# One kernel, one change: gate and value products of batch 0 on 16-bit parts, and the scores of a pair's first two row blocks issued in one run

## The chip, the cores and the metric

The kernel runs on one core of a Trainium2 chip. Its engines are TensorE (PE, whose weight loads the profile lists apart as PEld), VectorE (DVE), ScalarE (ACT), GpSimd (POOL) and SyncE (SP, whose queue issues the transfers). The metric is the time of one execution in device microseconds, the median of several runs.

## What is computed

Four batches of 576 tokens, 8 heads of 64. Inputs are 32-bit floats, and the result must hold about that precision.

```python
scores = q @ k.T / 8, causal;  a = softmax(scores);  local = a @ v
phi(x) = where(x > 0, x, exp(x) - 1) + 1
mem = (phi(q) @ M_prev) / (phi(q) . z_prev + 1e-6)
x  = g * mem + (1 - g) * local              # g = sigmoid(beta) per head; 512 columns
h  = (x @ w1) * (x @ w2)                    # 1024 columns
x2 = (h @ w3) @ moe_w_out                   # 512 columns
y  = (sigmoid(x2 @ w_gate) * (x2 @ w_val)) @ moe2_w_out   # 1536 columns inside, 512 out
```

## The kernel before

**Stages.** For each batch, `attention(b)` makes x, and `ffn(b)` goes through four stages that the trace calls `ab` (x times w1 and w2, f = 0 to 7), `xw` (h times the product of w3 and w_out, which is made once at the start, `wps`; d = 0 to 3), `gv` (gate and value, f = 0 to 11) and `ot` (output). Attention of batch b+1 is interleaved with `ffn(b)`: `drive` (L1376) steps the attention generator at the `yield`s of the feed-forward loops. The `gv` loops have no `yield` inside, so no attention is interleaved there. PE's order is the order in which the program issues (`manual_schedule`, L1441); the other engines' orders, and SP's, come from a scheduler that simulates the program.

**Precise products.** A 32-bit matrix is split into a high part and the rest, and each block product is three matmuls (high x high, low x high, high x low; `prod`, L519). In batch 0 all parts are 32-bit (`split_rows`, L720: a cast on ACT, a subtraction on DVE). From batch 1 on, gate and value use 16-bit parts that are scaled by a power of two first (`split_scaled`, L178: ACT makes the high part, DVE the low one). The power comes from the largest magnitude: `largest` gives maxima per partition, `total` (L168) adds these over the partitions by a matmul with a matrix of ones, and `power` (L158) takes four small DVE steps from it. Batches 2 and 3 use a scheme with fewer products (`two_rows`), for which sums of weight blocks are prepared too.

**Weights.** They arrive as 64-bit words. `conv_step` (L379) turns half a unit into 32-bit floats (two ACT passes and one on DVE), takes the maximum of gate/value, ab and o2 units, stores a 32-bit copy (`kept`; `kf`, `ko` in the trace) and issues the load of the half three further on. A unit of gate and value is the 8 blocks of 128 x 128 for one f. `split_step` (L458) then splits a half into a slot of the ring `wslot` (five slots of 4 KB per partition). A unit of batch 0 so takes two slots. `conv_step` runs at most two units ahead of `split_step`. `pump` (L489) calls one late step, one `conv_step` and one `split_step` after every second block product of `prod`, that is after six matmuls.

**Late tasks.** When all units are converted, `late_step` works through `tasks` (L243): it reloads a kept copy (`wrawl`), makes the scaled 16-bit parts "P", the block sums, and their parts "S" (`late_split`, L321), and stores them for the batches to come. The list starts with the P parts of the 12 gate/value units, then the six of o2, then the eight ab units (P, sums, S), then the S parts of gate/value, then of o2. `limit` says how far the list may be worked in a stage, `pace` after how many pumps a piece is done. The scales of all these weights are made in one go after gate/value of batch 0 (`late_scales`, L311), o2's at the start of batch 1 (L762).

**Scores.** `s_part` (L1146) issues the scores of one row block i of a pair of heads, 116 rows by 116 (i + 1) columns, for both heads of the pair at once: three terms of two matmuls of 64 rows each, into the two PSUM banks "s", which DVE then reads with the mask and a running minimum (L1174). The fifth row block is done in two runs of 290 columns. After it come exp on ACT, the normalisation on DVE or POOL, and transposes into the one bank "t".

Of the kernel before, what the change touches and what calls it, by code (L numbers as in the profile page):

```python
# [32 lines left out]
PB = 5  # L33
# [30 lines left out]
def tile_attention_memory_ffn(  # L64
# [178 lines left out]
    tasks = [(u, "P") for u in jobs[:F2]] + [(("o", *x), "P") for x in pairs_of]  # L243
# [28 lines left out]
    ws = {"conv": 0, "step": 0, "split": 0, "ring": 0, "freed": 0, "use": 0, "again": 0, "pumps": 0, "late": 0, "task": 0, "part": 0, "limit": 0, "pace": 0, "tops": 0, "wo": 0, "pass": 0, "wready": False}  # L272
    tmp = {}

# [46 lines left out]
    def late_split():  # L321
# [5 lines left out]
        late_o2 = u not in rank  # L327
        by = o2s[:, 0:1] if late_o2 else wsc[:, rank[u] : rank[u] + 1]
# [50 lines left out]
    def conv_step():  # L379
# [27 lines left out]
        elif ws["step"] == 1:  # L407
# [7 lines left out]
            if u in rank:  # L415
# [42 lines left out]
    def split_step():  # L458
# [5 lines left out]
        u, hf = divmod(s, 2)  # L464
        r = raws[u][:, 4 * hf : 4 * hf + 4, :]
# [28 lines left out]
    def need(store, s):  # L494
        while s not in store:
            moved = split_step()
            moved = conv_step() or moved
            assert moved
# [216 lines left out]
    def gvw(b, s, w, k):  # L715

        m = (k + 2 * w) % 4
        return (slot(s), 4 * w + m) if b else (slot(s + w), m)

# [37 lines left out]
    def ffn(b):  # L757
# [3 lines left out]
        if b == 1:  # L761
            o2_scale()  # L762
            ws["limit"], ws["pace"] = NFIRST, PACE[5]
        if b == 2:
            ws["pace"] = PACE[3]
        if b > 0:
            htop = fp.tile([128, F1], F32, tag="htop", name=f"htop{b}", bufs=1)
        for f in range(F1):
# [36 lines left out]
            if b > 0:  # L805
                largest(htop[:, f : f + 1], hraw, AX.X)

# [11 lines left out]
        for d in range(KC):  # L819
            if b > 0 and d == 1:  # L820
                x2back = finish_x2(b, x2s)
                if b == 1:
                    split_scaled(x2[0][:, 0], x2[0][:, 1], x20, x2s[:, 0:1])
            s = take(2)
            if b < 2:
                xt = fp.tile([128, 2, S], F16 if b else F32R, tag=f"x{d}", name=f"x2_{b}_{d}", bufs=1)
                x2.append(xt)
            if b == 1 and d == 0:
                x20 = fp.tile([128, S], F32, tag="hraw", name="x20")
            for n, hf in enumerate((1, 0) if b > 1 and d == KC - 1 else (0, 1)):  # L830
                c0 = hf * HS
                ps = ps_f.tile([128, 512], F32, tag="f", name=f"xw{b}_{d}_{hf}")
# [7 lines left out]
                if b == 0:  # L840
                    nc.scalar.copy(xt[:, 0, c0 : c0 + HS], ps[:, :HS])
                    nc.vector.tensor_sub(
                        xt[:, 1, c0 : c0 + HS], ps[:, :HS], xt[:, 0, c0 : c0 + HS].bitcast(F32)
                    )
                elif b == 1 and d == 0:
                    nc.scalar.copy(x20[:, c0 : c0 + HS], ps[:, :HS])
                elif b == 1:
# [37 lines left out]
        if b == 1:  # L885
            ws["limit"], ws["pace"] = NPARTS, PACE[1]
# [14 lines left out]
        for f in range(F2):  # L901
# [41 lines left out]
            s = take(1 if b else 2)  # L943
            for hf in range(2):
                c0 = hf * HS
                pss = []
                for w in range(2):
                    ps = ps_f.tile([128, 512], F32, tag="f", name=f"gv{b}_{f}_{hf}_{w}")
                    pss.append(ps)
                    for k in range(KC):  # L950
                        prod(ps[:, :HS], *gvw(b, s, w, k), x2[k], c0, k == 0, k == KC - 1)
                        if k % 2 == 1:
                            pump()
                    if w == 0:
                        asb = fp.tile([128, HS], F32, tag="asb", name=f"gsb{b}_{f}_{hf}")
                        act_fn(out=asb, in_=ps[:, :HS], func=AF.Sigmoid, scale=x2back[:, f : f + 1] if b else 1.0)
                    if hf == 1 and (b == 0 or w == 1):
                        release(s + (w if b == 0 else 0))
                if b:
                    nc.vector.scalar_tensor_tensor(  # L960
                        hraw[:, c0 : c0 + HS], pss[1][:, :HS], x2back[:, f : f + 1], asb, ALU.mult, ALU.mult
                    )
                else:
                    nc.vector.tensor_mul(hraw[:, c0 : c0 + HS], pss[1][:, :HS], asb)
# [6 lines left out]
        if b == 0:  # L971
            late_scales()
            ws["limit"], ws["pace"] = F2, PACE[0]
# [59 lines left out]
    def finish_x2(b, x2s):  # L1033
        power(x2s[:, 0:1], x2s[:, 1:2], total(f"x2sum{b}", bcol[:, B + b : B + b + 1]))
        back = fp.tile([128, F2], F32, tag="x2back", name=f"x2back{b}", bufs=1)
        nc.vector.tensor_scalar(back, wsc[:, NJ : NJ + F2], x2s[:, 1:2], None, ALU.mult)
# [29 lines left out]
    def attention(b, lag):  # L1066
# [79 lines left out]
        def s_part(p, i, n):  # L1146
            w = T * (i + 1)
            if n == 0:
                ps_ = []
                for hh in range(2):  # L1150
                    name = f"p{b}_{p}_{i}_{hh}"
                    if first and np_["n"] % 2 == 0:
                        m = np_["n"] // 2 % P0
                        ps_.append(fp.tile([T, 2 * S], F32, tag=f"h{m}", name=name, bufs=1)[:, :SP])
                    else:
                        ps_.append(ap.tile([T, SP], F32, tag="p", name=name, bufs=PB))
                    np_["n"] += 1
                sp[p, i] = (ps_, ap.tile([T, 8], F32, tag="sm", name=f"sm{b}_{p}_{i}", bufs=6))
# [362 lines left out]
```

## Time and profile before

| What | Before |
|---|---|
| Median of three runs (lowest, highest) | 1017.32 us (1014.89, 1017.9) |
| The profiled execution's own time | 1013.13 us |
| Its span, from first to last instruction | 1011.3 us |
| PE busy, PEld busy | 97%, 79% of the span |
| DVE, ACT, POOL busy | 72%, 59%, 19% of the span |
| Transfers | 227 MB, 225 GB/s on average |
| Granted TensorE clock | 0.995 of full speed |

All positions are microseconds from the start of the span of one profiled execution. "Busy" of an engine is the time in which at least one of its instructions was running; overlapping ones count once. Durations of matmuls are longer than the distance from one to the next, since they are pipelined; the pace is read from the busy time of a group over its count. Stages of batch 0: `ab` from 117.9, `xw` from 219.1, `gv` from 257.3, `ot` from 334.1; of batch 1: `ab` from 385.7, `xw` to 499.5, `gv` to 570.3, `ot` to 622.

### The profile page before, as it was taken

Reading aid. Unit: us, or ns where it says so; the run is one execution under the profiler, and the core shown is the slowest. Engines: PE = TensorE matmul, PEld = TensorE weight load, DVE = VectorE, ACT = ScalarE, POOL = GpSimd, SP = SyncE. Lnnn points to the kernel's source line nnn. Section 1 sums busy time; section 2 is a strip of 40 time slices with the busy share of each in tenths; the row PEclk is TensorE's granted clock in tenths of the full one; section 3 lists DMA queues with packets and bytes.
Section 4 is the critical chain, followed back from the end, with each engine's and each line's share of the span. In section 5 each row is a group of like instructions: output and inputs, shape, how many; then the busy total and the mean of one; then the engine's idle time right before and its main releaser. Section 6 shows DMA issues by size and latency. Waiting matters only on the chain. (4 is left out here: it accounts for less than half of the span.)

```text
span 1011.3 us, 19894 instructions
## 1 busy us (share of the span) xinstructions
PE 982.4 (97%) x7351; PEld 797.9 (79%) x7351; DVE 731.3 (72%) x1702; ACT 596.6 (59%) x1213; POOL 195.0 (19%) x196
## 2 busy tenths in 40 slices
PE   7999999999999999999999999999999999999998
PEld 3556687888999898898977777778777667797776
DVE  6866788777778826777777668988876757737883
ACT  7987787567777735564654545555655545324451
POOL 3454012213000101312200011343111311201110
PEclk9989999999999999999999999999999999999999
DMA  8865799967777249877887576655655556556532
GB/s 293 245 230 192 247 346 310 326 206 254 249 250 247 98 137 380 286 226 238 297 310 261 176 251 240 214 190 184 200 181 178 185 157 204 186 174 246 183 131 79
DMA packets 95642, 227.21 MB, mean 225 GB/s; under 512 B 11192, under 2 KB 39992, under 8 KB 95288
## 3 DMA queue, kind: packets, MB, share of 16 engines
q1 hardware_dynamic: 95544, 225.93, 66.3%
q8 instruction: 58, 0.95, 0.4%
q14 instruction: 40, 0.33, 0.1%
HBM read 164.55 MB, written 61.34 MB: 223 GB/s over the span
## 5 line engine op out<-in xcount | busy, mean ns | idle before, releaser
L532 PEld LDWEIGHTS <-wslot 128*128 128x128 f16 x1680 | 162.9, 98 | 49.7 <-issue 8.3
L1200 POOL TENSOR_SCALAR p<-p,sm,omg 116x116 f32<-116x116 f32 (+4 forms) x100 | 89.0, 895 | 406.2 <-DVE sm L1198 294.9
L521 PE MATMUL gv<-x,wslot 128*128 128x288 f32 (+1 forms) x1152 | 147.5, 290 | 0.2 <-ACT gsb L137 0.2
L521 PEld LDWEIGHTS <-wslot 128*128 128x128 f16 x1152 | 111.1, 98 | 32.1 <-issue 4.5
L532 PE MATMUL gvp<-x,wslot 128*128 128x288 f16 x1008 | 125.2, 286 | 3.6 <-ACT x L180 1.6
L137 ACT ACTIVATE p<-p,sm 116x116 f32<-116x116 f32 (+4 forms) x160 | 93.2, 585 | 46.6 <-DVE sm L1174 46.5
L521 PE MATMUL ot<-hg,wslot 128*128 128x288 f16 (+1 forms) x864 | 118.1, 291 | 0.0
L521 PE MATMUL ab<-x,wslot 128*128 128x288 f32 x768 | 117.2, 302 | 0.5 <-ACT asb L800 0.3
L521 PE MATMUL xw<-h,wslot 128*128 128x288 f32 x768 | 113.0, 300 | 1.7 <-ACT h L721 1.0
L521 PEld LDWEIGHTS ab<-x,wslot 128*128 128x128 f32 x768 | 104.0, 188 | 6.3 <-issue 2.9
L521 PEld LDWEIGHTS xw<-h,wslot 128*128 128x128 f32 x768 | 103.4, 188 | 5.5 <-issue 2.0
L1174 DVE CUSTOM_DVE_ANT_0 p<-s,msk 116x116 f32<-116x116 f32 (+4 forms) x160 | 68.0, 452 | 30.8 <-PE s L1169 26.8
L532 PE MATMUL abp<-x,wslot 128*128 128x288 f16 x672 | 87.1, 286 | 1.3 <-DVE u2ab L603 1.1
L723 DVE TENSOR_TENSOR wslot<-wraw,wslot 128x512 fp32r<-128x512 f32 x76 | 54.9, 725 | 34.7 <-ACT wslot L721 34.4
L521 PEld LDWEIGHTS gv<-x,wslot 128*128 128x128 f32 x576 | 76.4, 188 | 0.5 <-ACT gsb L137 0.5
L1230 PE MATMUL t<-idf,p 116*116 116x116 f32 x480 | 68.7, 272 | 3.3 <-DVE p L1200 2.5
L1230 PEld LDWEIGHTS t<-idf,p 116*116 116x116 f32 x480 | 54.3, 139 | 18.0 <-issue 5.3
L402 ACT ACTIVATE cy<-r 128x512 f32<-128x512 f32 x76 | 51.5, 678 | 13.3 <-DVE wraw L411 2.6
L721 ACT CAST wslot<-wraw 128x512 fp32r<-128x512 f32 x76 | 47.1, 621 | 16.2 <-PE gv L521 7.4
L411 DVE SCALAR_TENSOR_TENSOR wraw<-cy,cr 128x512 int32<-128x512 int32 x76 | 54.2, 740 | 2.6 <-ACT cr L403 2.1
L521 PE MATMUL wps<-wo,wslot 128*128 128x512 f32 x192 | 52.2, 407 | 0.0
L1248 ACT COPY pt<-t 116x696 f32<-116x696 f32 (+2 forms) x74 | 47.5, 650 | 7.4 <-PE t L1230 7.1
(210 smaller groups left out, 1630.0 us busy)
## 6 DMA issues: line engine op xcount, KB each, us to landing
wslot<-k SPq DMA_DIRECT2D x40, 512.0 KB, 4.3
wslot<-ka SPq DMA_DIRECT2D x40, 512.0 KB, 4.4
wrawl<-kf SPq DMA_DIRECT2D x32, 512.0 KB, 6.1
wslot<-kb SPq DMA_DIRECT2D x40, 384.0 KB, 3.5
k<-wslot SPq DMA_DIRECT2D x24, 512.0 KB, 4.7
r<-in_gv_dram SPq DMA_DIRECT2D x24, 512.0 KB, 5.1
kf<-wraw SPq DMA_DIRECT2D x20, 512.0 KB, 3.5
ka<-wS SPq DMA_DIRECT2D x20, 512.0 KB, 4.4
```

Source lines behind the costliest of these rows:

```text
L137: ins = nc.scalar.activation(**kw)
L402: nc.scalar.activation(out=y, in_=hi, func=AF.Prelu, scale=2.0**-112, alpha=2.0**32)
L411: nc.vector.scalar_tensor_tensor(z, y, 3, tmp["r"], ALU.logical_shift_left, ALU.bitwise_or)
L521: paced["pe"] = nc.tensor.matmul(ps, w[:, wi, blk, :], x[:, xi, cols : cols + n], start=first and part == 0, stop=last and part == 2,)
L532: paced["pe"] = nc.tensor.matmul(ps, w[:, wi, blk + k, :], x[:, xi, k, :], start=not more and k == 0 and part == 0, stop=k == 1 and part == 2,
L721: nc.scalar.copy(dst[:, 0], src)
L723: eng.tensor_sub(dst[:, 1], src, dst[:, 0].bitcast(F32))
L1174: nc.vector.tensor_tensor_reduce(out=ps_[hh][:, c0:c1], in0=os_[hh], in1=msk[:, SP - w + c0 : SP - w + c1], scale=-0.125, scalar=3.0e38 if ...
L1200: lower(SHARE_N).tensor_scalar(ps_[hh][:, :w], ps_[hh][:, :w], sm[:, 6 + hh : 7 + hh], omg[:T, 2 * p + hh : 2 * p + hh + 1], ALU.mult, ALU ...
L1230: nc.tensor.transpose(tp[:T, c : c + T], src[hh][:, j * T : (j + 1) * T], idf[:T, :T])
L1248: nc.scalar.copy(to, got)
```

## The change

Gate and value units are now split once, at conversion, into scaled 16-bit parts of the whole unit: `scaled_step` waits until both halves are converted, issues the unit's own scale (`unit_scale`: two one-column products of ones into the bank "t", then `power`) at least four pumps after the last conversion, and at a later pump the split of all 1024 columns into one slot, whose store for the later batches is issued at once. The 12 P tasks of gate/value leave the late list, `late_scales` keeps only ab's scales, and o2's scale moves to the first late o2 task. x2 of batch 0 becomes scaled 16-bit parts as in batch 1: the bound on it needs a maximum of every h (two for each of the last four f) and the maxima of the w3-w_out product. Gate/value of batch 0 then runs as in batch 1 (one slot a unit, a scale in the sigmoid and in the product). In attention of batches 1 to 3, `s_part` issues row blocks 0 and 1 together, side by side in the same two banks, and returns at once for row block 1; score buffers become six, and q's tile gets a single buffer. The limits of the late list follow: o2's P parts during the output stage of batch 0, ab's parts from the start of batch 1, the S parts of gate/value from the gate/value stage of batch 1.

```diff
-PB = 5
+PB = 6
...
-    def total(name, *cols):
+    def total(name, *cols, bank=None):
         n = cols[0].shape[1]
-        ps = ps_f.tile([128, 512], F32, tag="f", name=name)
+        ps = (bank or ps_f).tile([128, 512], F32, tag="t" if bank else "f", name=name)
...
-    tasks = [(u, "P") for u in jobs[:F2]] + [(("o", *x), "P") for x in pairs_of]
+    tasks = [(("o", *x), "P") for x in pairs_of]
...
     def late_scales():
-        power(wsc[:, :NJ], wsc[:, NJ:], total("wsum", mcol[:, 0, :NJ], mcol[:, 1, :NJ]))
-        nc.vector.tensor_reduce(wmax, wtop.rearrange("p d f -> p f d"), AX.X, ALU.max)
+        power(wsc[:, F2:NJ], wsc[:, NJ + F2 :], total("wsum", mcol[:, 0, F2:NJ]))
...
+    def unit_scale(u):
+        n = rank[u]
+        power(wsc[:, n : n + 1], wsc[:, NJ + n : NJ + n + 1], total(f"wsum{n}", *(mcol[:, hf, n : n + 1] for hf in range(2)), bank=ps_t))
+        scaled.add(u)
+
+    def scaled_step(u, now):
+
+        if ws["conv"] < 2 * u + 2:
+            return False
+        if u not in scaled:
+            if not now and ws["pumps"] < ws["ready"]:
+                return False
+            unit_scale(u)
+            return True
+        if in_use("wslot") >= RING:
+            return False
+        w = fp.tile([128, 2, 8, 128], F16, tag="wslot", name=f"wslot{ws['ring']}", bufs=RING)
+        split_scaled(w[:, 0], w[:, 1], raws.pop(u), wsc[:, rank[u] : rank[u] + 1])
+        nc.sync.dma_start(out=whole16[u]["P"], in_=w)
+        done.append((u, "P"))
+        put("wslot", [w])
+        ws["split"] += 2
+        return True
...
+        if late_o2 and "o2" not in scaled:
+            scaled.add("o2")
+            o2_scale()
+            return
...
+                ws["ready"] = ws["pumps"] + 4
             ws["step"] = 0
             ws["conv"] += 1
...
+        if u in rank and rank[u] < F2:
+            return scaled_step(u, now)
...
         if b == 1:
-            o2_scale()
-            ws["limit"], ws["pace"] = NFIRST, PACE[5]
+            ws["limit"], ws["pace"] = NPARTS, PACE[5]
...
-            if b > 0:
+            if b > 0 or f >= F1 // 2:
                 largest(htop[:, f : f + 1], hraw, AX.X)
+            if b == 0 and f >= F1 // 2:
+                m = f - F1 // 2
+                largest(htop[:, m : m + 1], hs[m][:, 0].bitcast(F32), AX.X)
...
+                if b == 0 and d == 0 and n == 1:
+                    while ws["tops"] < KC:
+                        assert conv_step() or split_step()
+                    nc.vector.tensor_reduce(wmax, wtop.rearrange("p d f -> p f d"), AX.X, ALU.max)
+                    x2s = bound_x2(b, htop)
...
         if b == 1:
-            ws["limit"], ws["pace"] = NPARTS, PACE[1]
+            ws["limit"], ws["pace"] = NSUMS, PACE[1]
...
-            s = take(1 if b else 2)
+            s = take(1)
+            if b == 0:
+                slot(s)
+                nc.vector.tensor_mul(x2back[:, f : f + 1], wsc[:, NJ + f : NJ + f + 1], x2s[:, 1:2])
...
-            ws["limit"], ws["pace"] = F2, PACE[0]
+            ws["limit"], ws["pace"] = NFIRST, PACE[0]
...
-                q_ = ap.tile([128, NT, 2, D], F32, tag="qnr", name=f"qnr{b}_{p}")
+                q_ = ap.tile([128, NT, 2, D], F32, tag="qnr", name=f"qnr{b}_{p}", bufs=1)
...
+            if i == 1 and not first:
+                return
+            rows = (0, 1) if i == 0 and not first else (i,)
+            jobs = []
+            at = 0
+            for i in rows:
...
+                jobs.append((i, w, c0, c1, at))
+                at += c1 - c0
...
+            for i, w, c0, c1, at in jobs:
+                for x, (q_, k_) in enumerate(terms):
+                    for hh in range(2):
+                        r = slice(64 * hh, 64 * hh + 64)
+                        nc.tensor.matmul(
+                            os_[hh][:, at : at + c1 - c0], q_[r, 0, i * T : (i + 1) * T], k_[r, 1, c0:c1],
+                            start=x == 0, stop=x == len(terms) - 1,
+                        )
+            for i, w, c0, c1, at in jobs:
+                ps_, sm = sp[p, i]
                 for hh in range(2):
...
```

## Rows read from the trace of the kernel before

**Rows 1.** The page's part 1: busy us (share) x instructions, whole span

```profile
PE 982.4 (97%) x7351; PEld 797.9 (79%) x7351; DVE 731.3 (72%) x1702; ACT 596.6 (59%) x1213; POOL 195.0 (19%) x196
```

**Rows 2.** Busy time by stretch: length, PE, PEld, DVE, ACT, POOL, PEclk, DMA share, GB/s

```profile
174.00:219.00 45.00, 44.64 (x347) 40.25 (x346) 32.43 (x80) 26.18 (x59) 8.46 (x8) 1.00 0.78 267
219.00:257.30 38.30, 36.64 (x285) 32.59 (x284) 30.66 (x75) 26.79 (x58) 9.86 (x8) 1.00 0.75 261
257.30:334.10 76.80, 76.56 (x578) 76.26 (x578) 60.36 (x108) 58.25 (x110) 0.00 (x0) 1.00 0.72 244
334.10:385.70 51.60, 50.44 (x376) 46.51 (x374) 24.42 (x51) 24.94 (x44) 6.00 (x4) 0.97 0.41 137
385.70:499.50 113.80, 113.09 (x880) 101.21 (x878) 84.22 (x223) 67.96 (x146) 30.91 (x27) 1.00 0.82 279
499.50:570.30 70.80, 70.80 (x581) 56.57 (x580) 51.95 (x90) 39.43 (x55) 0.00 (x0) 1.00 0.81 270
570.30:622.00 51.70, 50.38 (x418) 37.35 (x417) 35.74 (x79) 26.64 (x46) 4.98 (x5) 1.00 0.63 210
498.00:515.00 17.00, 17.00 (x140) 13.82 (x139) 11.51 (x19) 9.21 (x13) 0.17 (x1) 1.00 1.04 365
```

**Rows 3.** Groups by form, whole span: busy us, mean ns | idle before

```profile
L521 PE MATMUL gv<-x,wslot 128*128 128x288 f32 x576 | 76.7, 295 | 0.2 <-ACT gsb L137 0.2
...
L521 PE MATMUL gv<-x,wslot 128*128 128x288 f16 x576 | 70.8, 286 | 0.0
```

**Rows 4.** Timeline of PE in batch 1's gate/value stage: start, us, what

```profile
517.15 0.17 PE L172 MATMUL hgsum<-bcol,ones 128*128 128x1 bf16 x1
517.18 0.65 PE L521 MATMUL gv<-x,wslot 128*128 128x288 f16 x4
```

**Rows 5.** DVE's groups by form, 257.3 to 334.1 (gate/value of batch 0)

```profile
L723 DVE TENSOR_TENSOR wslot<-wraw,wslot 128x512 fp32r<-128x512 f32 x24 | 16.5, 687 | 14.3 <-ACT wslot L721 14.3
L176 DVE TENSOR_REDUCE mcol<-wraw 128x1 bf16<-128x512 f32 x24 | 16.3, 680 | 0.0
L411 DVE SCALAR_TENSOR_TENSOR wraw<-cy,cr 128x512 int32<-128x512 int32 x24 | 15.4, 682 | 0.0
L964 DVE TENSOR_TENSOR hgraw<-gv,gsb 128x288 f32<-128x288 f32 x23 | 10.3, 448 | 2.1 <-ACT gsb L137 1.7 <-PE gv L521 0.4
L723 DVE TENSOR_TENSOR hg<-hgraw,hg 128x576 fp32r<-128x576 f32 x11 | 8.2, 747 | 0.0
```

**Rows 6.** Groups by form, whole span, of operations that batch 0 takes over

```profile
L181 DVE SCALAR_TENSOR_TENSOR wP<-wrawl,wsc,wP 128x1024 f16<-128x1024 f32 x12 | 15.7, 1305 | 11.6 <-ACT wP L180 11.0 <-DMA wslot<-k 0.5
...
L960 DVE SCALAR_TENSOR_TENSOR hgraw<-gv,x2back,gsb 128x288 f32<-128x288 f32 x24 | 12.4, 516 | 11.5 <-PE gv L521 9.6 <-PE hgsum L172 1.5 <-ACT gsb L137 0.4
```

**Rows 7.** Line 163, a step of `power`: duration ns min/median/max

```profile
L163 DVE TENSOR_SCALAR pw<-x2sum x3: 144/157/158, 475.5 to 893.6; 128x1 int32<-128x1 int32 x3
```

**Rows 8.** DMA issues by line: count, KB each, median us to landing

```profile
r<-in_gv_dram SPq DMA_DIRECT2D x24, 512.0 KB, 5.1
...
kb<-wP SPq DMA_DIRECT2D x12, 512.0 KB, 6.1
```

**Rows 9.** Timelines of PE around score visits in ab of batches 1 and 2

```profile
386.30 0.31 PE L1169 MATMUL s<-qkh 64*116 64x116 f32 x2
...
386.75 2.64 PE L521 MATMUL ab<-x,wslot 128*128 128x288 f32 x18
389.32 0.36 PE L1169 MATMUL s<-qkh 64*116 64x232 f32 x2
...
389.82 0.66 PE L521 MATMUL ab<-x,wslot 128*128 128x288 f32 x3
...
623.38 4.58 PE L532 MATMUL abp<-x,wslot 128*128 128x288 f16 x36
627.90 0.37 PE L1169 MATMUL s<-qkh 64*116 64x232 f32 x2
```

**Rows 10.** Timeline of PE in ot of batch 0, with [idle before <-releaser]

```profile
347.06 0.90 PE L1169 MATMUL s<-qkh 64*116 64x290 f32 x2 [1.16 <-DVE sm L1174]
```

More of the change, by code (lines that the diff above doesn't have):

```diff
@@ L271, in tile_attention_memory_ffn @@
     wot = {}
-    ws = {"conv": 0, "step": 0, "split": 0, "ring": 0, "freed": 0, "use": 0, "again": 0, "pumps": 0, "late": 0, "task": 0, "part": 0, "limit": 0, "pace": 0, "tops": 0, "wo": 0, "pass": 0, "wready": False}
+    ws = {"conv": 0, "step": 0, "split": 0, "ring": 0, "freed": 0, "use": 0, "again": 0, "pumps": 0, "late": 0, "task": 0, "part": 0, "limit": 0, "pace": 0, "ready": 0, "tops": 0, "wo": 0, "pass": 0, "wready": False}
     tmp = {}
+    scaled = set()
     last = {}
@@ L456, in load_step, with split_step @@
         return True
-    def split_step():
+    def split_step(now=False):
         s = ws["split"]
@@ L819, in ffn @@
         for d in range(KC):
[L820 removed]
+            if d == 1:
                 x2back = finish_x2(b, x2s)
[L822 removed]
+                if b < 2:
                     split_scaled(x2[0][:, 0], x2[0][:, 1], x20, x2s[:, 0:1])
@@ L955, in ffn @@
                         asb = fp.tile([128, HS], F32, tag="asb", name=f"gsb{b}_{f}_{hf}")
[L956 to L964, printed above, removed]
+                        act_fn(out=asb, in_=ps[:, :HS], func=AF.Sigmoid, scale=x2back[:, f : f + 1])
+                    if hf == 1 and w == 1:
+                        release(s)
+                nc.vector.scalar_tensor_tensor(
+                    hraw[:, c0 : c0 + HS], pss[1][:, :HS], x2back[:, f : f + 1], asb, ALU.mult, ALU.mult
+                )
             if b:
@@ L1159, in s_part @@
-            ps_, sm = sp[p, i]
-            c0, c1 = (0, w) if w <= 512 else ((0, SP // 2), (SP // 2, SP))[n]
-            os_ = []
-            for hh in range(2):
-                ps = ps_s.tile([128, 512], F32, tag="s", name=f"s{b}_{p}_{i}_{n}_{hh}")
-                os_.append(ps[:T, : c1 - c0])
-            terms = [(qks[p], qks[p])] if first else [(parts[p][x], parts[p][y]) for x, y in ((0, 0), (1, 0), (0, 1))]
-            for x, (q_, k_) in enumerate(terms):
-                for hh in range(2):
-                    r = slice(64 * hh, 64 * hh + 64)
-                    nc.tensor.matmul(
-                        os_[hh], q_[r, 0, i * T : (i + 1) * T], k_[r, 1, c0:c1],
-                        start=x == 0, stop=x == len(terms) - 1,
-                    )
@@ L1173, in s_part @@
-            for hh in range(2):
-                nc.vector.tensor_tensor_reduce(
-                    out=ps_[hh][:, c0:c1],
-                    in0=os_[hh],
-                    in1=msk[:, SP - w + c0 : SP - w + c1],
-                    scale=-0.125,
-                    scalar=3.0e38 if n == 0 else sm[:, 2 * hh : 2 * hh + 1],
-                    op0=ALU.add,
-                    op1=ALU.min,
-                    accum_out=sm[:, 2 * hh + n : 2 * hh + n + 1],
-                )
+            if i == 1 and not first:
+                return
@@ new lines, in s_part @@
+            os_ = [
+                ps_s.tile([128, 512], F32, tag="s", name=f"s{b}_{p}_{i}_{n}_{hh}")[:T, :at] for hh in range(2)
+            ]
+            terms = [(qks[p], qks[p])] if first else [(parts[p][x], parts[p][y]) for x, y in ((0, 0), (1, 0), (0, 1))]
+            for i, w, c0, c1, at in jobs:
+                for x, (q_, k_) in enumerate(terms):
+                    for hh in range(2):
+                        r = slice(64 * hh, 64 * hh + 64)
+                        nc.tensor.matmul(
+                            os_[hh][:, at : at + c1 - c0], q_[r, 0, i * T : (i + 1) * T], k_[r, 1, c0:c1],
+                            start=x == 0, stop=x == len(terms) - 1,
+                        )
```

60 lines of the change are left out of this document (31 added, 29 removed).

## The prediction

> **What bounds the kernel now.** I read the page's busy line first: TensorE is busy 982.4 of 1011.3 us [rows 1], so only what shortens or interrupts TensorE's own stream counts. Then the busy time by stage [rows 2]. In the gate/val stage of batch 0 (257.3 to 334.1) PE is busy 76.56 of 76.8 us, DVE 60.36, ACT 58.25, and the transfers run at 244 GB/s with a share of 0.72: it is PE-bound, but the other engines have only a fifth to spare. The same 576 products of batch 1 (499.5 to 570.3) fill 70.8 us, also without idle time. The groups by form say why [rows 3]: 576 products with 32-bit parts are 76.7 us of PE, 133 ns each; with 16-bit parts 70.8 us, 123 ns each.
>
> **Part 1, 16-bit gate/val products.** 76.7 - 70.8 = -5.9 us if nothing else stands in the way. Twelve scale sums of two one-column products are new in PE's stream; before such a product 0.03 us pass until the next big one starts [rows 4], so 12 x 2 x 0.03 = +0.7 us.
>
> The same DVE must now serve a faster PE. Its work for one unit while one unit is consumed, by mean durations [rows 5 to 7]: two conversions (2 x 682), two maxima (2 x 680), one split of 1024 columns (1305, in place of 2 x 687), four small steps for the power of two and one for the product with x2's scale (5 x about 155), two evictions that now take a scale (2 x 516, in place of 2 x 448), one split of hg (747): 6.58 us, against 5.74 now. Durations overlap at their ends: the groups of rows 5 add up to 66.7 us, with 0.6 of smaller ones 67.3, where DVE is busy 60.36 [rows 2], a factor of 0.90. So 5.9 us per unit against PE's 48 x 0.123 + 0.06 = 5.96: no room where a unit is made for each one used; now it is 5.15 of 6.38. Not all units are such: the ring of five slots holds five 16-bit units where it held two and a half, so about three more are made in the stage of xw, where DVE is busy 30.66 of 38.3 us. Of the twelve some seven are left, then o2 units follow, whose two half splits and conversions cost as now. DVE also waits in order for ACT's half of a split, 14.3 us in 24 splits here [rows 5], but while ahead of PE. I charge 0.2 us to each of the seven, +1.5 us. Bounds: 0 (batch 1 has DVE at 51.95 of 70.8 us and PE without a gap) and +5.9 (the stage stays as long as it is), or more in the second rival.
>
> Twelve stores of 512 KB [rows 8] move from the late tasks to this stage, on the SP queue behind each split and ahead of the next raw load; the 12 reloads that fed those tasks vanish. A unit moves 244 GB/s x 6.38 us = 1.56 MB now, 2.08 MB then: 2.08 MB / 5.96 us = 349 GB/s, where the stretch from 498 to 515 us carries 365 GB/s at a share of 1.04 [rows 2]. A raw load is issued three halves ahead, some 9 us, and lands in 5.1 us [rows 8], so I cost it at nothing; if landings doubled, ACT would stand before the conversion and the gate behind it.
> The Trainium skill (DMA: Bandwidth & Descriptors, Specifications) gives about 358 GB/s as the HBM limit of one core and so speaks against putting these stores here; by it, an estimate, a unit could not take less than 2.08 / 358 = 5.8 us, the sum would stay, and only bursts would cost something. The 365 GB/s of the row differ little from it; I let it speak for the first rival below.
>
> **Part 2, x2 of batch 0 scaled.** Eight more maxima of h, each at 576/512 of the 680 ns that one of 512 columns takes [rows 5], are 6 us of DVE in the last four f of ab, where it is busy 32.43 of 45 us [rows 2]: hidden, and 6 us would be the price without cover. The chain behind h (a product, a sum, a copy, one product of ones, four power steps) sits in the second half of d = 0, with 24 products of 133 ns and attention to hide it; +0.3, bounds 0 and +2. Three to five scale sums fall into the xw stage and share one bank with attention's transposes, which then also wait for DVE's reading; +0.5, bounds 0 and 5 x 0.7 = +3.5 (0.7 us being a DVE piece of 680 ns ahead of that reading).
>
> **Part 3, rows 0 and 1 of a pair in one run.** In the timeline [rows 9] a visit of 116 columns lasts 386.75 - 386.30 = 0.45 us until the next ab product starts, one of 232 columns 389.82 - 389.32 = 0.50 us. The 18 ab products between them take 389.32 - 386.75 = 2.57 us, where 18 x 0.133 are 2.39: 0.18 us go to leaving and re-entering. Two visits cost 0.45 + 0.50 + 2 x 0.18 = 1.31 us. One run: 0.18 + 0.50 + three more terms, whose starts stand 0.10 to 0.15 us apart, 0.36: 1.04 us. That is -0.27 us a pair beside 32-bit products; beside 16-bit ones 36 products take 627.90 - 623.38 = 4.52 us, 0.09 over 36 x 0.123, so -0.17. Batches 1 to 3 have 12 pairs, nine beside 32-bit products: -2.9 at most, and as the first pairs run before 219 us, where PE is not always the bound, I take -2.4; bounds -3.3 and 0 (the reductions of a run take four turns on DVE, but the next visit is some 7 us later). The sixth score buffer and the single q buffer cost nothing: a buffer is taken again only after its transposes, one row earlier in PE's own order, and q's readers are done early in a pair.
>
> **Part 4, the late tasks.** Twelve P tasks leave, 1.3 us of DVE each, and all that follow move up: six o2 tasks and the o2 scale into the output stage of batch 0 (DVE 24.42 of 51.6 us), the three-part ab tasks into ab and xw of batch 1 (DVE 84.22 of 113.8 us, some 10 us more), the second sums of gate/val into its gate/val stage. PE has 0.7, 0.0 and 1.3 us idle in the three stages of batch 1 [rows 2], so relief buys little: -0.5, bounds -2 and +2. One stall that this reshuffles stands alone: PE waits 1.16 us for a score reduction at 347 us [rows 10]; at once afterwards the granted clock falls to its lower level for a while: 0.97 on average over 51.6 us is 3.1 us at 1.2 in place of 2.4 GHz, 1.55 us lost. It may go or come back elsewhere: 0, bounds -2.7 and +2.7.
>
> **Sum.** -5.9 + 0.7 + 1.5 + 0.3 + 0.5 - 2.4 - 0.5 = -5.8 us. The profiled execution took 1013.1 us (span 1011.3 and 1.8 around it), 1.8 under the fastest of the runs shown; so 1007.3 on its scale, and 1017.3 - 5.8 = 1011.5 on that of the median.
>
> **Rivals.**
> First, the stage keeps its old length: DVE (5.9 of 5.96 us) and the queue (349 of 365 GB/s) hold PE at 6.38 us a unit. For it: both margins are under 5%; against it: three units made ahead, and the o2 part is lighter. Left is +0.3 + 0.5 - 2.4 - 0.5 = -2.1: 1015.2.
> Second, slower: PE stands at the scale sums. Each is issued four pumps, 24 products or 2.95 us, after the last conversion step of its unit; that step and its maximum take DVE 1.36 us, so from 1.6 us of delay on DVE the in-order PE stops there, its evictions stop with it, and neither can run ahead to absorb the waits between ACT and DVE. A unit then costs 5.9 + 14.3/12 = 7.1 us, for the seven and two more at the start 9 x 1.1 = +9.9, and one fall of the clock +1.55: 71.5 + 11.5 - 76.7 = +6.3, less 2.1: +4.2, 1021.5. For it: DVE at 5.9 of 5.96; against it: in batch 1 the one scale product in the middle of the stage made no gap.
> Third, more gain: the seven units cost nothing, and the wait at 347 us goes with its fall of the clock, -1.5 - 2.7: 1007.3.
> That the edit doesn't do what it says I exclude for the form of the products; for the visits it is the 0 of part 3.
>
> **How the numbers follow.** Forecast 0.47, first rival 0.25, second 0.17, third 0.11. What a measurement can tell here is 0.3%, 3.05 us: forecast and third are faster (0.58), the first is within (0.25), the second slower (0.17). The range holds the forecast with both neighbours, 1006 to 1019; left out are most of the second rival and the third's tail.
>
> **What would show it.** Gate/val of batch 0 with 576 products at 98 ns a load and 123 ns apart, the stage near 73 us; waits of PE for DVE at the scale sums under 0.2 us each; 12 runs of 12 score products; P tasks of gate/val gone from 373 us on, with 12 stores between 220 and 330 us. I am wrong if the stage is no shorter than 76 us, if PE waits for maxima or the transposes' bank over 3 us in all, or if the time comes from batches 2 and 3.

## The result, and the profile after

The change made the kernel slower. The changed kernel took 1022.21 us (median of 16 runs, 1016.33 to 1026.48), the kernel before 1015.72 us on the same chip (16 runs, 1010.64 to 1019.88): ratio 1.0059, 95% interval [1.0044, 1.0075]. The forecast was 1011.5 us and faster. The profiled execution of the changed kernel took 1026.5 us (span 1024.7), 4.3 above its median, so what its stages lose is the upper end of what the change costs.

The page's busy line of the changed kernel, to be read beside [rows 1]:

```profile
PE 982.6 (96%) x7375; PEld 783.1 (76%) x7375; DVE 738.5 (72%) x1752; ACT 587.2 (57%) x1190; POOL 192.3 (19%) x196
```

TensorE is as busy as before, in a span 13.4 us longer: it stood 13 us more. Nor is its busy time the same work: in all it ran 34.1 us at the lower level of its clock (1.2 of 2.4 GHz), where before ran 10.2.

The stages, by TensorE's first products of each, in us; two profiled executions of each kernel (the second ones are the runs e17 and e4 below):

| Stage | Before, two executions | Changed, two executions |
|---|---|---|
| start (`wps`) | 89.5, 92.2 | 91.0, 90.9 |
| `ab` of batch 0, f = 0 to 3 | 65.4, 66.4 | 73.5, 74.0 |
| `ab` of batch 0, f = 4 to 7 | 35.8, 35.8 | 39.6, 38.5 |
| `xw` of batch 0 | 38.2, 38.4 | 43.3, 43.5 |
| `gv` of batch 0 | 76.9, 76.9 | 74.9, 75.2 |
| `ot` of batch 0 | 51.6, 50.0 | 49.5, 49.5 |
| `ab` of batch 1 | 80.8, 80.3 | 79.0, 79.0 |
| `xw`, `gv`, `ot` of batch 1 | 155.5, 155.5 | 155.1, 155.1 |
| `ab` of batch 2 | 59.4, 59.4 | 63.2, 63.2 |
| `xw`, `gv`, `ot` of batch 2 | 163.4, 163.4 | 161.1, 161.1 |

The gains are some 7 us in all: in `gv` and `ot` of batch 0, in batch 1, and in the last stages of batch 2. Those last 2.3 us are more than the merged visits were to give there: the visits alone (e1 below) have 0.8 of them, the 16-bit products alone (e2) 2.1. The losses stand in `ab` and `xw` of batch 0 (some 16 us) and in `ab` of batch 2 (3.8). Busy time by stretch of the changed kernel (length, PE, PEld, DVE, ACT, POOL, PEclk, DMA share, GB/s): f = 0 to 3 and f = 4 to 7 of `ab`, `xw`, `gv`, `ot`, and `ab` with `xw` of batch 1, beside [rows 2]:

```profile
119.00:192.50 73.50, 65.92 (x420) 54.04 (x419) 57.45 (x129) 50.52 (x106) 10.16 (x11) 0.93 0.88 316
192.50:232.10 39.60, 37.25 (x281) 33.47 (x279) 27.52 (x64) 19.73 (x47) 5.27 (x5) 0.96 0.61 195
232.10:275.40 43.30, 39.62 (x289) 34.86 (x290) 34.92 (x97) 29.27 (x58) 9.47 (x8) 0.92 0.73 259
275.40:350.30 74.90, 72.03 (x598) 56.97 (x596) 66.85 (x148) 60.87 (x103) 0.00 (x0) 1.00 0.89 325
350.30:399.80 49.50, 48.88 (x374) 45.07 (x373) 23.00 (x50) 22.71 (x40) 5.96 (x4) 1.00 0.41 136
399.80:511.20 111.40, 111.03 (x879) 100.35 (x878) 86.25 (x227) 62.73 (x142) 31.97 (x27) 1.00 0.70 230
```

The first four f of `ab` in the kernel before, the same columns:

```profile
117.90:183.30 65.40, 62.29 (x420) 51.17 (x419) 54.90 (x128) 49.99 (x106) 11.76 (x11) 1.00 0.97 343
```

The same 420 matmuls take 8.1 us longer: TensorE idles 7.6 us in place of 3.1, and its clock is granted at 0.93 of full speed. The waits in that stretch (engine, line, waited for: total us, times, longest), first before, then changed:

```profile
PE t L1230 <- DVE p L1200: 2.3, 2, 1.5
```
```profile
PE t L1268 <- DVE p L1238: 6.8, 2, 4.4
```

The longest of them, 4.4 us, is a wait of TensorE for VectorE's normalisation of a row block. The other, 2.4 us at 128.56, comes with the merged visits: e1 and e6 below have it too (2.7 and 2.9 us), and take 65.5 and 66.8 us for this stretch. TensorE's timeline of the changed kernel shows the wait of 4.4 us, and the stretches on either side what the clock did:

```profile
151.77 3.68 PE L552 MATMUL wps<-wo,wslot 128*128 128x512 f32 x15
159.87 0.61 PE L1268 MATMUL t<-idf,p 116*116 116x116 f32 x2 [4.41 <-DVE p L1238]
```
```profile
155.00:160.00 5.00, 0.59 (x4) 0.20 (x3) 4.53 (x9) 2.04 (x5) 2.33 (x2) 0.93 0.85 299
160.00:166.00 6.00, 6.00 (x26) 3.40 (x28) 4.14 (x10) 1.57 (x4) 0.54 (x1) 0.50 0.98 299
```

TensorE stood 4.4 us, and then ran 6.0 us at the lower level, which is 3.0 us more lost. VectorE's order at that place:

```profile
150.77 0.75 DVE L176 TENSOR_REDUCE htop<-h 128x1 f32<-128x576 f32 x1
151.43 0.27 DVE L1212 CUSTOM_DVE_ANT_0 p<-s,msk 116x116 f32<-116x116 f32 x1
...
153.59 0.69 DVE L774 TENSOR_TENSOR wpart<-wps,wpart 128x512 f32<-128x512 f32 x1
154.19 0.16 DVE L1235 TENSOR_SCALAR sm<-sm 116x2 f32<-116x2 f32 x1
154.26 0.82 DVE L1138 SCALAR_TENSOR_TENSOR mphi<-qnr,me 116x640 f32<-116x640 f32 x1
154.99 0.69 DVE L749 TENSOR_TENSOR wslot<-wraw,wslot 128x512 fp32r<-128x512 f32 x1
155.60 0.16 DVE L1236 RECIPROCAL sm<-sm 116x2 f32<-116x2 f32 x1
155.67 1.43 DVE L1235 TENSOR_SCALAR sm<-sm 116x2 f32<-116x2 f32 x1
157.57 0.69 DVE L774 TENSOR_TENSOR wpart<-wps,wpart 128x512 f32<-128x512 f32 x1 [0.47 <-DMA wpart<-wp]
158.18 1.28 DVE L439 SCALAR_TENSOR_TENSOR wraw<-cy,cr 128x512 int32<-128x512 int32 x2
159.38 0.34 DVE L1238 TENSOR_SCALAR p<-p,sm,omg 116x116 f32<-116x116 f32 x1
```

The first line is one of the eight new maxima, of h1. Its input has been there for long, so the scheduler put it early, just ahead of the two row blocks' score reductions. The normalisation (last line) comes behind an addition of partial sums that waits for its reload, and behind two conversions. It has its reciprocal at 155.76, and runs 3.6 us later.

### The profile page after: what moved, and what is told of

Read it like the earlier page. It is cut to its first block, busy times and chain, and to the rows that moved or that the text cites. A ratio compares the mean times of both kernels' runs of the same rounds, so it can differ in the third digit from the quotient of the medians.

```text
span 1024.7 us, 19911 instructions
## 1 busy us (share of the span) xinstructions
PE 982.6 (96%) x7375; PEld 783.1 (76%) x7375; DVE 738.5 (72%) x1752; ACT 587.2 (57%) x1190; POOL 192.3 (19%) x196
## 5 line engine op out<-in xcount | busy, mean ns | idle before, releaser
L552 PEld LDWEIGHTS <-wslot 128*128 128x128 f16 x1728 | 166.9, 98 | 48.7 <-issue 7.3
L563 PEld LDWEIGHTS <-wslot 128*128 128x128 f16 x1680 | 163.1, 98 | 53.0 <-issue 11.6
L1238 POOL TENSOR_SCALAR p<-p,sm,omg 116x116 f32<-116x116 f32 (+4 forms) x100 | 86.1, 865 | 375.4 <-DVE sm L1236 288.4
L552 PE MATMUL gv<-x,wslot 128*128 128x288 f16 x1152 | 142.6, 286 | 2.6 <-ACT gsb L137 1.4
L137 ACT ACTIVATE p<-p,sm 116x116 f32<-116x116 f32 (+4 forms) x160 | 92.9, 583 | 39.8 <-DVE sm L1212 39.6
L552 PEld LDWEIGHTS ab<-x,wslot 128*128 128x128 f32 x768 | 106.9, 193 | 5.0 <-issue 3.1
L1268 PE MATMUL t<-idf,p 116*116 116x116 f32 x480 | 69.0, 275 | 10.2 <-DVE p L1238 8.8
L749 DVE TENSOR_TENSOR wslot<-wraw,wslot 128x512 fp32r<-128x512 f32 x52 | 38.3, 739 | 21.7 <-ACT wslot L747 20.0
L1336 PE MATMUL o<-pt,vs 116*64 116x344 f32 (+2 forms) x320 | 51.2, 427 | 0.0
L431 ACT ACTIVATE cr<-r 128x512 int32<-128x512 uint32 x76 | 50.6, 665 | 0.0
```

Of the source, the lines that this page charges most:

```text
L137: ins = nc.scalar.activation(**kw)
L431: nc.scalar.activation(out=r, in_=w[:, :, 0].bitcast(U32), func=AF.Copy, scale=LAST3, bias=HALF)
L552: paced["pe"] = nc.tensor.matmul(ps, w[:, wi, blk, :], x[:, xi, cols : cols + n], start=first and part == 0, stop=last and part == 2,)
L563: paced["pe"] = nc.tensor.matmul(ps, w[:, wi, blk + k, :], x[:, xi, k, :], start=not more and k == 0 and part == 0, stop=k == 1 and part == 2,
L749: eng.tensor_sub(dst[:, 1], src, dst[:, 0].bitcast(F32))
L1238: lower(SHARE_N).tensor_scalar(ps_[hh][:, :w], ps_[hh][:, :w], sm[:, 6 + hh : 7 + hh], omg[:T, 2 * p + hh : 2 * p + hh + 1], ALU.mult, ALU ...
```

## The experiments

Ratios are to the kernel before on the same chip. "First four f" is that part of `ab` of batch 0: 65.4 and 66.4 us before, 73.5 changed.

**The parts alone.** e1 is before with the merged visits (and their six score buffers and single q buffer), e2 the changed kernel with separate visits and the old buffers, e3 before with the new buffer counts alone, e4 the changed kernel once more.

The buffer counts, which e1 and e3 take over, and the line of the merged visits, which e1 takes over and e2 takes back:

```diff
-PB = 5
+PB = 6
...
-                q_ = ap.tile([128, NT, 2, D], F32, tag="qnr", name=f"qnr{b}_{p}")
+                q_ = ap.tile([128, NT, 2, D], F32, tag="qnr", name=f"qnr{b}_{p}", bufs=1)
...
+            rows = (0, 1) if i == 0 and not first else (i,)
...
```

> The kernel before with only the scores of row blocks 0 and 1 in one run, with the six score buffers and the single q buffer that go with it. If the merged visits cost the time (four score reductions in a row on DVE, so the normalisation and PE's transposes behind it come late): about +6 us against before, with PE waiting for the normalisation in ab of batch 0. If the single q buffer costs it: +6 us here and the same with the buffers alone. If gate/value on 16-bit parts costs it: -2.4 us here, as part 3 of the prediction had it.

> The changed kernel with the scores as before (two visits), five score buffers and two q buffers, so gate/value on 16-bit parts alone. If the merged visits or the single q buffer cost the time: -2 to -4 us against before (the stage of gate/value 2 us shorter and the output stage 2 us). If gate/value's own additions cost it (eight maxima in ab, the scale of x2, the scale sums in xw): +6 to +8 us, with batch 0's ab and xw 10 us longer as in the changed kernel's trace.

> The kernel before with six score buffers and a single q buffer, nothing else. If SP's queue stands at the load of q until DVE has read the pair before, and holds the raw weight loads behind it: +4 to +8 us, with waits of SP at that load. By both other theories: within 2 us of before.

> The changed kernel itself on the same chip as the three before, for comparison: +6 us against before by the runs known so far (+0.44 to +0.75%). If the parts add up, it is the sum of the first two of these runs; if the parts hinder each other, more than that sum.

Measured: e1 0.9997 [0.9978, 1.0016], e2 1.0024 [1.0011, 1.0036], e3 1.0047 [1.0031, 1.0064], e4 1.0099 [1.0064, 1.0135]. The parts don't add: 0 and +0.24% alone, +0.6 to +1.0% together. The first four f took 65.5 us in e1, 66.0 in e2 and 66.4 in e3, so neither part alone loses them.

**The q buffer, and the maxima.** e5 is the changed kernel with two q buffers (and one of `qt`, for room), e8 the merged visits alone with the same. e6 holds the eight maxima of h until the last product of their own f; e7 leaves them out, with a constant in their place. The edit of e6:

```diff
-                largest(htop[:, f : f + 1], hraw, AX.X)
+                ins = largest(htop[:, f : f + 1], hraw, AX.X)
+                if b == 0:
+                    behind(ins)
...
-                largest(htop[:, m : m + 1], hs[m][:, 0].bitcast(F32), AX.X)
+                behind(largest(htop[:, m : m + 1], hs[m][:, 0].bitcast(F32), AX.X))
```

> The changed kernel with two q buffers again, and the transposed q (read only until the next pair's fourth row) in one buffer in exchange. If the single q buffer costs what the buffers alone cost on the kernel before (+0.5%): 5 us less than the changed kernel, about +2 to +4 us against before, and ab of batch 0 some 6 us shorter than its 73.5 us. If it is the maxima: as the changed kernel, +6 to +10.

> The changed kernel with the eight maxima of h in batch 0 held, in the scheduler's order only, behind the last product of their f, so that DVE does not take the first ones at 135 and 150 us, between the scores and the normalisation that PE waits for. If these early maxima delay the normalisation: the wait of PE of 4.8 us at 155 us goes, the first half of ab of batch 0 is back at 66 us from 73.5, and the time is 6 to 8 us less than the changed kernel's. If the single q buffer is the cause: no difference from the changed kernel.

> The changed kernel without the eight maxima: the bound on x2 of batch 0 comes from a constant (4.0) in place of the measured |h|. If DVE's 6 us for them are the price: ab of batch 0 back at 101 us from 113, and -8 us against the changed kernel. If only their place was wrong: the same as with late maxima. If neither, the cause is in the scores' visits or the buffers: no difference.

> The kernel before with the scores in one run, six score buffers, two q buffers and one buffer of transposed q. If the single q buffer hid the gain of the merged visits (buffers alone +0.47%, with the visits -0.03%): 4 to 5 us faster than before. If the visits' own gain is the 2.4 us of the prediction: -2 to -3 us. If the two were noise of the order: no difference.

Measured: e5 1.0063 [1.0041, 1.0084], e6 0.9992 [0.9975, 1.0009], e7 0.9988 [0.9973, 1.0002], e8 1.003 [1.0013, 1.0047]. The q buffer isn't the cause: a second one gains nothing. (In e5 the wait at the row block is 1.3 us in place of 4.4 and the first four f take 70.1 us, and yet the time stays; more on this below.) The maxima are: held late, the same eight operations cost nothing that can be measured against leaving them out, and the first four f are back at 66.8 us (65.7 in e7). So it is their place, not their 6 us. VectorE's order in e6 at the same row block:

```profile
150.48 0.17 DVE L1237 TENSOR_SCALAR sm<-sm 116x2 f32<-116x2 f32 x1
150.55 0.69 DVE L774 TENSOR_TENSOR wpart<-wps,wpart 128x512 f32<-128x512 f32 x1
151.15 0.16 DVE L1238 RECIPROCAL sm<-sm 116x2 f32<-116x2 f32 x1
151.22 0.81 DVE L1140 SCALAR_TENSOR_TENSOR mphi<-qnr,me 116x640 f32<-116x640 f32 x1
151.94 0.34 DVE L1240 TENSOR_SCALAR p<-p,sm,omg 116x116 f32<-116x116 f32 x1
```

The normalisation (last line) stands directly behind `mphi`, 1.5 us after its first step (the first line) and ahead of the second addition; TensorE's only long wait in that stage is another one, the 2.9 us at 124.90 that come with the merged visits.

**What goes with what.** e9 is e1 plus the eight maxima, early, their results unused. e10 is e2 with the maxima held. e11 and e12 were meant to be faster than before: e6 with the scale sums in the bank "f", and e6 with five score buffers and two q buffers. The edit of e9, against e1:

```diff
-        if b > 0:
+        if True:
...
-            if b > 0:
+            if b > 0 or f >= F1 // 2:
                 largest(htop[:, f : f + 1], hraw, AX.X)
+            if b == 0 and f >= F1 // 2:
+                m = f - F1 // 2
+                largest(htop[:, m : m + 1], hs[m][:, 0].bitcast(F32), AX.X)
```

> The kernel of the merged scores alone (ratio 0.9997 to before), plus the same eight maxima of h at the places that they have in VectorE's order in the changed kernel; their results are used by nothing. Theory (the early maxima push row block 0's normalisation behind a reload in VectorE's order, and merged visits make TensorE stand there): the first four f of ab go from 65.5 us to about 72 to 74, the clock falls there, and the time is 0.4 to 0.9% above the scores alone, about 1020 to 1024 where before stands at 1016. Rival (the early maxima cost only together with the 16-bit gv, its conversions or its extra transposes): the first four f stay at 65 to 67 us and the ratio at 1.000 to 1.002.

> The 16-bit gv alone (two score visits, ratio 1.0024) with the eight maxima of batch 0 held until the last product of their f. Theory: with two visits the place of the maxima hardly matters (the first four f were 66.0 us already), so the ratio stays at 1.000 to 1.003. Rival (the maxima cost wherever they stand early): ratio falls by 0.5% or more, to 0.996 to 0.998, with shorter ab and xw of batch 0.

> The changed kernel with the eight maxima held late (ratio 0.9992), and the scale sums in the output bank f in place of the transposes' bank t. Theory: what is left of the longer xw (42.1 us against 38.2) is in part the wait of the first scale sum for the bank t, about 1.1 us, so xw goes to 40.5 to 41.5 and the ratio to 0.997 to 0.999. Rival (the fall of the clock at the entry of xw makes all of it): xw stays at 42 and the ratio at 0.999 to 1.000; a dearer wait for the bank f at the end of gv would show as a ratio above 1.000.

> The changed kernel with the eight maxima held late (ratio 0.9992), with five score buffers and two q buffers as before the change. Theory (six score buffers and one q buffer cost what they cost by themselves, 0.47%): the ratio falls to 0.995 to 0.997, about 1011 where before stands at 1016, with the third batch's ab back from 63.2 to about 60 to 61.5 us. Rival (any other order of VectorE's work lengthens that stage, whatever the buffers): it stays at 62.5 to 63.5 us and the ratio at 0.998 to 1.001.

Measured: e9 1.0118 [1.0093, 1.0143], with the first four f at 74.6 us; e10 1.0009 [0.9987, 1.003], with 66.2; e11 1.0009 [0.9986, 1.0033], e12 1.0099 [1.0074, 1.0125]. e9 settles what the cause needs: merged visits (with the buffer counts that they bring; early maxima with these counts alone were not tried) and early maxima, and nothing of the 16-bit products. In its trace TensorE stands at the same place, and the stretch behind it runs below full clock:

```profile
162.22 0.61 PE L1243 MATMUL t<-idf,p 116*116 116x116 f32 x2 [4.78 <-DVE p L1213]
```
```profile
162.30:169.00 6.70, 6.70 (x44) 4.24 (x44) 4.20 (x10) 1.61 (x4) 0.53 (x1) 0.75 0.97 287
```

e11 takes the bank away as a reason for the longer `xw`: it stays at 42.2 us (and `gv` takes 77.3 us there, against 74.6 in e6). e12's theory fell: its third `ab` is 64.0 us, and its loss is spread over the start (93.0), the first `ab` and `xw` in other waits; another buffer count makes another order.

**One operation, and one order.** Of e15, e14 and e13: e15 is e1 with the maximum of h1 alone, unused; e14 the changed kernel with that one maximum held; e13 the changed kernel with all maxima early, but the partial sums' additions ordered behind the last normalisation. e16 is e13 again, e17 before again. The edit of e14, then that of e13:

```diff
-                largest(htop[:, m : m + 1], hs[m][:, 0].bitcast(F32), AX.X)
+                ins = largest(htop[:, m : m + 1], hs[m][:, 0].bitcast(F32), AX.X)
+                if m == 1:
+                    behind(ins)
...
-                nc.vector.tensor_add(part, ps, part)
+                add = nc.vector.tensor_add(part, ps, part)
+                if "n" in paced:
+                    behind(add, "n")
...
-                lower(SHARE_N).tensor_scalar(
+                ins = lower(SHARE_N).tensor_scalar(
...
+                paced["n"] = ins
```

> The changed kernel, with all maxima where they are and one order tied: in VectorE's order the additions of partial sums in ab come behind the last normalisation issued before them, so row block 0's normalisation of the second pair stands two places ahead of the addition that waits for its reload instead of three behind it. Theory (that place is the whole of the first ab stage's loss): TensorE's wait of 4.4 us and the fall of the clock behind it go, the first four f take 65.5 to 68 us in place of 73.5, start unchanged near 91 us, ratio to before 0.999 to 1.002, from 1.006 to 1.010. Rival (the maxima's time on VectorE, or the fall of the clock without the wait): the first four f stay at 71 to 74 us, ratio 1.005 or more.

> The changed kernel with one of the eight maxima held, that of h1 (0.75 us at 150.8 us); the other three early ones stay early. Theory (this one turns the order at row block 0): the first four f take 65.5 to 68 us, start near 91 us, ratio 0.999 to 1.002. Rival (each early maximum takes its share): a quarter of the loss goes, the first four f at 71 to 72 us, ratio about 1.005.

> The kernel of the merged scores alone (ratio 0.9997) plus one single maximum, that of h1, early in VectorE's order; its result is used by nothing. Theory (one operation of 0.75 us turns the order, TensorE stands 4 to 5 us and its clock falls): the first four f go from 65.5 to 72 to 75 us, ratio 1.006 to 1.010. Rival (the eight together, with their 6 us, make it): 65.5 to 67 us, ratio 1.000 to 1.002.

> The kernel of e13 once more. In its profiled execution, 1027.7 us where the median was 1019.5, TensorE stood 2.7 us for a score reduction near 140 us, some 15 us ahead of the place that the kernel changes. If that wait belongs to that execution and not to the order: the first four f take 66 to 70 us here, with under 2.5 us of wait at row block 0's transposes of the second pair and no wait over 2 us near 140; the median stays near 1019. If it belongs to the order: 72 to 73 us again.

> The kernel before itself, for the spread of a stage between executions. If stages repeat: start 89 to 90, first four f of ab 65 to 66, ab of the third batch 59 to 60 us, and a ratio of 1.000 with its interval across it. If the start or the third batch's ab come out 2 us or more apart, what is read from single profiles there (5.4 us in the start of e6, 3.8 us in that ab) says nothing of the change.

Measured: e15 1.0063 [1.0039, 1.0088] and 73.2 us; e14 1.0018 [0.9995, 1.0041] and 65.9; e13 1.0046 [1.0021, 1.007] and 72.8; e16 1.0049 [1.0031, 1.0068] and 67.2; e17 1.0011 [0.9992, 1.003] and 66.4. TensorE at the row block's transposes in e1 (no wait), in e15, then in e16:

```profile
156.49 0.36 PE L1240 MATMUL t<-idf,p 116*116 116x116 f32 x2
```
```profile
158.24 0.61 PE L1242 MATMUL t<-idf,p 116*116 116x116 f32 x2 [3.85 <-DVE p L1212]
```
```profile
157.16 0.57 PE L1271 MATMUL t<-idf,p 116*116 116x116 f32 x2 [1.61 <-DVE p L1240]
```

One unused operation of 0.75 us brings the wait back (e15, +0.7% over e1), and taking it out of its place removes it (e14). Of e15's 7.6 us some 2.2 are another wait, for a score reduction at 136 us (2.6 us, 0.3 in e1), which e11 and e13 have too (2.5 and 2.4 us) and e16 hasn't: it comes and goes between executions of one kernel. In the profiled execution of e14, 3 us above its median, only the first four f come back; f = 4 to 7 take 40.5 us and `xw` 43.3, where e6 has 36.9 and 42.1.

e13 and e16 change the order alone: the wait at the row block falls from 4.4 to 1.6 us, in e16 no fall of the clock follows, and the stage is back at 67.2 us; in e13 that other wait and two falls kept it at 72.8, where its rival had it. Yet both give back only about 0.1% of the time against the changed kernel's 1.0059, inside its interval (0.5% against the 1.0099 of e4), and e5, with a wait of 1.3 us, gives back none. The mean granted clock of all their executions gives a hint: it is 0.988 to 0.989 in e5, e13 and e16, as in the changed kernel (0.988), 0.990 in e6, e7 and e14, and 0.992 to 0.994 in before, so in most executions of the three the falls seem to have stayed. In the profile the mechanism is shown; how much of the median this one wait makes stays open. What the early place of the maxima costs by any way is measured: e6, e7 and e14 (0.4 to 0.7% less than the changed kernel) and e9 and e15 (0.7 to 1.2% more than e1) put it at 4 to 12 us.

No version beat the kernel before by more than can be told: e7 and e6 stand at 0.9988 and 0.9992.

## Why the prediction was wrong

**The step that failed** is in part 2: "Eight more maxima of h ... are 6 us of DVE in the last four f of ab ... hidden, and 6 us would be the price without cover". I looked for room by the busy time of one stretch, and took the place of the operations from the place in the program. The four maxima of h0 to h3 are issued in the last four f, but the scheduler, which sees their inputs ready, put them at 135.7, 150.8, 178.1 and 195.2 us, three of them in the first four f, where VectorE was busy 54.90 of 65.40 us and TensorE's in-order transposes wait on it. Nor was the price the 6 us: a displaced 0.75 us operation turned the order of one on the path. I had no rival for that. The second rival had its kind right (TensorE in order behind VectorE, then a fall of the clock) but the wrong place: waits for the power of two at the scale sums of `gv` are 0.3 us in all. That its time, 1021.5 us, is near the measured 1022.2 is luck: it had `gv` 6.3 us longer, and `gv` became some 2 us shorter.

The maxima are not all of the miss. Held or left out (e6, e7), they leave the kernel about 1 us under before, inside the interval, not 5.8: `xw` is still 3 to 4 us longer, and `ab` of batch 2 3.5 to 3.8.

**Falls of the clock** stood in the sum at nothing (part 4: 0, 2.7 either way), and at 1.55 us in that rival. Measured: in `ab` and `xw` of batch 0 the changed kernel ran 20.5 us at the lower level and before none, in either execution, which loses half of them, 10 us. The four falls there go with waits of TensorE of 2.4, 4.4, 2.0 and 1.5 us; the longest in these stages of before is 1.5. I priced delays by their length, where this wait and its fall cost 4.4 + 3.0. Over all executions the mean granted clock is 0.988 for the changed kernel, and 0.992 to 0.994 for before. Where TensorE is busy all the while this loses 12 us and 6 to 8 us, so the clock makes up to 4 to 6 of the 6.5 us between the medians.

**Part 1** had the mechanism right and the size half. `gv` of batch 0 went from 76.9 to 74.9 and 75.2 us, forecast 73.1 (76.8 - 5.9 + 0.7 + 1.5). The 576 products took 71.9 us of TensorE, against 70.8 in [rows 3], and TensorE stood 2.9 us, not 1.5. VectorE is busy 66.85 us, 6.5 more; the prediction's 0.75 us a unit (5.9 - 5.15) give 5.3 for the seven units it left to this stage, but ten of the twelve were split here (the count of the second group below), only two in `xw`. The transfers ran at 325 GB/s and a share of 0.89, which did not hold the stage as a whole; but ScalarE waited 2.8 us for raw loads of gate and value, which the prediction put at nothing and before shows none of, and TensorE's wait of 0.49 us at 314.92 stands behind one of these. Nor is the gain firm: in single executions of the kernels with these products `gv` took from 73.7 us (e14) to 76.6 (e7; 77.3 in e11 with its other bank). Groups of the stage, changed (out<-in, form, count | busy us, mean ns | idle before, ended by), beside [rows 5, 6]:

```profile
L552 PE MATMUL gv<-x,wslot 128*128 128x288 f16 x576 | 71.9, 286 | 2.6 <-ACT gsb L137 1.4 <-DVE hgraw L989 1.1
```
```profile
L181 DVE SCALAR_TENSOR_TENSOR wslot<-wraw,wsc,wslot 128x1024 f16<-128x1024 f32 x10 | 12.8, 1282 | 1.3 <-ACT wslot L180 1.2
L989 DVE SCALAR_TENSOR_TENSOR hgraw<-gv,x2back,gsb 128x288 f32<-128x288 f32 x23 | 11.8, 514 | 4.5 <-PE gv L552 2.5 <-ACT gsb L137 1.9
```

**Part 2's +0.8 for `xw`** (bank and chain) measured +5. The entry waits were there before (1.0 us for ACT's half and 0.7 for VectorE's, no fall of the clock behind them); in the changed kernel they are 1.5 and 1.3, and the clock falls right behind the first, with 7 us at 0.51 in which the second wait lies:

```profile
237.45 0.57 PE L552 MATMUL xw<-h,wslot 128*128 128x288 f32 x2 [1.52 <-ACT h L747]
239.36 0.61 PE L552 MATMUL xw<-h,wslot 128*128 128x288 f32 x1 [1.34 <-DVE h L749]
```
```profile
237.60:244.60 7.00, 5.66 (x26) 4.81 (x27) 4.41 (x17) 3.96 (x8) 1.75 (x2) 0.51 0.60 219
```

Both the maxima on top of the merged visits (e9, 42.0 us against 39.3 in e1) and the 16-bit parts without maxima (e7, 41.4) lengthen it, and the bank does not (e11). A wait of the first scale sum for ACT is 0.8 us.

**Part 3** held for a visit, not for the kernel: e1 is no faster than before (0.9997). One run of row blocks 0 and 1 in TensorE's timeline:

```profile
400.29 0.31 PE L1205 MATMUL s<-qkh 64*116 64x116 f32 x2
...
400.91 0.26 PE L1205 MATMUL s<-qkl,qkh 64*116 64x232 f32 x2
401.10 0.66 PE L552 MATMUL ab<-x,wslot 128*128 128x288 f32 x3
```

401.10 - 400.29 = 0.81 us for twelve matmuls, forecast 0.86 (0.50 + 0.36). In e1 the later stages gained 2.0 us (`ab` and `xw` of batch 1, `xw` and `ot` of batch 2), forecast 2.4. What it did not foresee is `ab` of batch 2, at 62.2 us in e1, against 59.4 in both executions of before. "The sixth score buffer and the single q buffer cost nothing" failed too: e3 is 0.47% slower, with 61.0 us there; where the rest of it is its trace doesn't show, being of its fastest execution. VectorE was busy 52.96 of 59.4 us in that stage of before, so I suspect that any new order shows; the waits of the changed kernel there are many and short, the largest two together 1.7 us. Which order causes them was not tried.

**Part 4** went as forecast in sign: batch 1 gained 1.6 us in `ab`, of which e1 has 0.7 by the visits alone. The stall at 347 us is there again in e17, of the same 1.16 us, but the clock stays at the full level behind it, and `ot` takes 50.0 us in place of 51.6: the fall, which I left at 0 with 2.7 us either way, belonged to one execution. The wait in e17, beside [rows 10]:

```profile
351.19 0.77 PE L1169 MATMUL s<-qkh 64*116 64x290 f32 x2 [1.16 <-DVE sm L1174]
```

## What to carry to other kernels

When operations are added to an engine whose order a scheduler makes, ask where it will put them (when their inputs are ready), not where they stand in the program, and who stands behind them on that engine with TensorE waiting in order. Tie operations that nobody needs soon to a late event: here that turned +0.6% into 0 without removing any work. Test parts alone and together: two edits that cost 0 and 0.24% alone cost 0.6% or more in one kernel.

## What the runs showed of the hardware

A wait of TensorE can cost more than its length: at the entry of `xw` the granted clock stayed at the full level behind the waits of 1.0 and 0.7 us of before, and in the changed kernel it fell behind the first wait, of 1.5 us, and was 0.51 for 7 us. Length alone does not decide it. In e1 waits of 0.8 and 0.7 us there were followed by a clock of 0.50 from 228.5 to 231.9; a wait of 1.6 us was followed by a fall in e13 and by none in e16, one kernel; and the 1.16 us in `ot` of batch 0 by a fall in one execution of before and by none in the other.

A VectorE operation on two numbers per partition took 1.43 us at 155.67 in place of 0.16, and ended at 157.10, 0.03 us after this operation of GpSimd, which had begun before it:

```profile
155.16 1.91 POOL L1140 TENSOR_TENSOR me<-mphi,z 116x640 f32<-116x640 f32 x1 [8.68 <-DVE mphi L1138]
```

The Trainium skill (SBUF — State Buffer, SBUF: two separate sides) says that VectorE and GpSimd share one pair of ports under an exclusive lock, and that whoever comes second blocks until the other's instruction ends; on VectorE's side it names operations in a 2-port mode and, against GpSimd operations that read SBUF, those with two SBUF inputs. The ends here agree. In which mode this operation ran the trace doesn't show, and no run here took the GpSimd operation away to test it. In e16 the normalisation itself fell into such an operation (1.55 us in place of 0.34).

Stages from `ab` of batch 1 to `ab` of batch 3 repeat to 0.6 us, but not those at the beginning: the start took 89.5 and 92.2 us in two executions of before, and the first four f of `ab` 72.8 and 67.2 in two of e13's kernel. The start took 91.2 us in e1 and 85.3 in e15, which differ by one operation behind it, and 85.6 in e6; so whole profiled spans of two kernels are not to be compared.
